# A linear attention and a mixture of sixteen experts in one kernel: thirteen products of ones between two batches of the first expert, and the second expert's first weights asked for earlier

## The chip, the cores and the metric

The kernel runs on one core of a Trainium2 chip. A core has a matrix engine (TensorE, PE in the profile; PEld is its loading of weights), a vector engine (VectorE, DVE), an engine for activations and copies (ScalarE, ACT), a general one (GpSimd, POOL) and SyncE (SP), which here only issues transfers. Transfers run on 16 DMA engines. The engines have queues of their own and wait for one another by semaphores. The metric is the device time of one execution, in microseconds (us).

## The reference

The first half is a recurrent attention over 4 sequences of 768 tokens, 8 heads of 48: a state of 48x48 per head is decayed by a weight per channel, and the outer product of key and value is added. The second half is a layer of experts for the 3072 tokens of 384 values. Each token picks one of 4 groups and one of 4 experts in it, by the greatest logit, and its result is scaled with both softmax weights.

```python
for t in range(S):
    cur = np.einsum('bhd,bhe->bhde', u[None] * kt, vt)
    y[:, :, t] = np.einsum('bhd,bhde->bhe', rt, state + cur)
    state = w[None, :, :, None] * state + np.einsum('bhd,bhe->bhde', kt, vt)
x = attn_out.transpose(0, 2, 1, 3).reshape(B * S, H * D)
g_idx = np.argmax(x @ w_group, axis=1)
...
e_idx = np.argmax(xg @ w_expert[g], axis=1)
...
h = np.maximum(xg[mask_e] @ w1[g, e], 0.0)
out[tok_idx] = combined[:, None] * (h @ w2[g, e])
```

An expert's weights are w1 of 384x1024 and w2 of 1024x384 in 32 bits, 1536 KB each.

## The kernel before, in words

**Attention and routing.** The sequences are worked through in 24 tiles of 128 tokens (six chunks of each of four sequences), in a loop over steps s (L852) whose order on each engine is the order in which the code is written. A tile is turned (`turn`), scored (`scores`), multiplied with the values (`values`) and brought back to rows (`back`) in successive steps. Behind that its logits are computed, and its tokens' expert, gate and place are found (`route`, L377). POOL then scatters the tile's rows by an indirect transfer (L457) into `x_sorted` in device memory, where each expert has a region of its own, in the order in which the tokens come. The last two scatters belong to the last two tiles.

**The experts begin before the routing has ended.** After 16 tiles (s = 21) `pick_first` has chosen the two experts with the most tokens so far; their numbers are loaded into SP as `first` and `second` (L894, L895). SP asks for the first expert's w1 (`load_w1`, L482: four transfers of 384 KB, 32 partitions each), later for the first 128 of its rows (`load_rows(0, ...)`, L933) and its w2 (`load_w2`, L488: one transfer of 1536 KB). The first expert's tokens are worked off in two batches of 128 (items 0 and 1); each of the other experts has one batch of 173 to 240 tokens (items 2 to 16).

**An item.** `columns` (L556) transposes its rows on DVE into `xe`. `up(i, f)` (L585) makes two of the eight row blocks of the hidden layer for f = 0, 2, 4, 6 (matmuls at L596), and ACT applies the rectifier (L600) into `hT`. `down(i, d)` (L605) makes one of three blocks of the result (matmuls at L617) into the tile `po`, and ACT copies it out (L620). ACT copies w2 in four parts into the order in which `down` reads it (`w2_part`, L477, the copies at L480). POOL scatters the results (L656).

**Where the weights lie.** Two places take turns. Place 0 (`w1`, `w2`) holds the first expert. Place 1 is laid over the rings that held k and r in the attention, `kall` and `rall`: the second expert's w1 goes into `kall`, its w2 into `rall`. The last reader of k in `kall` is POOL (L691).

**The order around the change.** PE's order: the last tile's end, `up(0, 4)`, `up(0, 6)`, `down(0, 0)`, `down(0, 1)`, `down(0, 2)`, then for item 1 `up(1, 0)` to `up(1, 6)` and `down(1, 0)`, then `up(2, 0)` and so on, with an item's last two `down` after the next item's first `up`. SP's order: `load_w2(first, 0)`; two of the four row transfers of item 1 (L963; the other two go from ACT) and its keys; four row transfers of item 2 and its keys (L987); the second expert's w1 and w2 (L988); then the third expert's rows and weights. The transfers of `x_sorted` rows to item 1 wait until all scatters into it have landed.

**Products that only use PE.** `warm(n)` (L201) multiplies a 128x128 tile of ones with itself n times into a PSUM bank called `idle`; the kernel calls it twice at its start (8 and 5 times). PSUM banks come in turn from a pool of six (`bank`, L90).

Of the kernel before, what the change touches and what calls it, by code (L numbers as in the profile page):

```python
# [15 lines left out]
P = 128  # L16
# [18 lines left out]
def kernel(  # L35
# [54 lines left out]
    def bank(shape, name):  # L90
        return psum.tile(shape, FP32, tag="bank", name=name)
# [106 lines left out]

    idle = bank([P, P], "idle")

    def warm(n):  # L201
        for _ in range(n):
            nc.tensor.matmul(idle, lhsT=ones, rhs=ones, start=True, stop=True)

# [87 lines left out]
    def turned(m):  # L292
# [5 lines left out]
        )  # L298

    warm(5)  # L300
    backwards(0, nc.vector)
    turned(0)
# [74 lines left out]
    def route(pool, rb, xt, T, sums, number, group, apart=False):  # L377
# [77 lines left out]
        def rows(i):  # L455
# [10 lines left out]
    places = [  # L466
        (wpool.tile([P, KO, F], FP32, name="w1"), wpool.tile([P, FO, DM], FP32, name="w2")),
        (
            kall.rearrange("p j a h d -> p (j a h d)").rearrange("p (k f) -> p k f", f=F),
            rall.rearrange("p j a h d -> p (j a h d)")[:, 0 : FO * DM].rearrange("p (k d) -> p k d", d=DM),  # L470
        ),
    ]
# [9 lines left out]
    def load_w1(e, i):  # L482
        for q in range(P // BL):
            nc.sync.dma_start(
                out=places[i][0][BL * q : BL * (q + 1)], in_=w1f[bass.ds(e, 1), q].rearrange("a p k f -> (a p) k f")
            )

    def load_w2(e, i):  # L488
        nc.sync.dma_start(out=places[i][1], in_=w2f[bass.ds(e, 1)].rearrange("a p k f -> (a p) k f"))

    def load_expert(e, i):

        load_w1(e, i)
        load_w2(e, i)
        return places[i]
# [15 lines left out]
    weights, xgs, xes, keys_of, hTs, yo = {}, {}, {}, {}, {}, {}  # L511

    def width(i):
        return ITEMS[i][2] - ITEMS[i][1]
# [4 lines left out]
    def item_tile(i, shape, name, dtype=FP32, bufs=2):  # L519
        return pools[min(i, 1)].tile(shape, dtype, tag=name, bufs=bufs if i > 0 else 1, name=name)  # L520

    def room(i):
        return P if i == 0 else CAP

    def is_last(i):
        return i == len(ITEMS) - 1

    def padded(n):
        return -(-n // BL) * BL

    def load_rows(i, expert, queue, other=None):

        def tl(shape, name):
            if i < 3:
                return pools[0].tile(shape, FP32, name=f"{name}_{i}")
            return pools[1].tile(shape, FP32, tag=name, bufs=3, name=name)

        n = room(i)  # L540
        xg, key = xgs[i] = tl([P, n // BL, KO, BL], "xg"), tl([P, n // BL, ROW_EXTRA], "key")
        a, w, rows = ITEMS[i][1], padded(width(i)), regions[bass.ds(expert, 1)]
        for q in range(P // BL):
            if other is not None and q % 2:
                of, by = regions[bass.ds(other[0], 1)], other[1]
            else:
                of, by = rows, queue
            by.dma_start(
                out=xg[BL * q : BL * (q + 1), 0 : w // BL].rearrange("t b k d -> t b (k d)"),
                in_=of[:, a : a + w, BL * KO * q : BL * KO * (q + 1)].rearrange("a (b t) d -> t (a b) d", t=BL),  # L550
            )
        p = P if is_last(i) else BL
        n = -(-w // p) * p
        queue.dma_start(out=key[0:p, 0 : n // p], in_=rows[:, a : a + n, DM:XW].rearrange("a (j p) w -> p (a j) w", p=p))

    def columns(i):  # L556
        xg = xgs[i][0]
        w = padded(width(i))
        xe = xes[i] = item_tile(i, [P, KO, room(i)], "xe")
        for ko in range(KO):  # L560
            nc.vector.transpose(xe[:, ko, 0:w].rearrange("p (b t) -> p b t", t=BL), xg[:, 0 : w // BL, ko, :])  # L561
# [43 lines left out]
    def down(i, d, beside=None):  # L605

        w = width(i)
        if d == 0:
            yo[i] = item_tile(i, [P, KO, room(i)], "yo")
            if w < padded(w):  # L610
                nc.vector.memset(yo[i][:, :, w : padded(w)], 0.0)  # L611
        hT, w2 = hTs[i], w2_parts[ITEMS[i][0] % 2]
        po = bank([P, w], "po")
        for fo in range(FO):
            if fo == FO // 2 and beside is not None:
                beside()
            nc.tensor.matmul(  # L617
                po, lhsT=w2[:, fo, d, :], rhs=hT[:, fo, 0:w], start=(fo == 0), stop=(fo == FO - 1)
            )
        nc.scalar.copy(yo[i][:, d, 0:w], po)  # L620
# [231 lines left out]
    for s in range(NT + LAST):  # L852
        pieces = todo.pop(s, [])

        def schedule(n):

            if n not in ROUTED:
                return
            choice, expert, exps, before, gate, place, rows = routing(n)
            if n == NT - 1:  # L860
                choice()
                expert()
                w2_part(0, 6, nc.scalar.copy)
                ending.extend((exps, before, gate, place, rows))
                return
            a = n + 4
            if n < NT - B - 1:
                when = [(a, "choice"), (a + 1, "choice"), (a + 1, "last"), (a + 2, "first")] + 2 * [(a + 2, "last")]
            elif n == NT - B - 1:
                when = [(a, "choice"), (a, "choice"), (a, "last")] + 3 * [(a + 1, "last")]  # L870
            else:
                when = [(a, "choice"), (a, "choice")] + 4 * [(a, "last")]
            for i in range(ROUTED[n]):
                when.append((when[5][0] + (1 + i if n < FOUR * B - 1 else 0), "last"))
            each = [lambda i=i: rows(i) for i in range(ROUTED[n])]
            for (at, place_in), part in zip(when, [choice, expert, exps, before, gate, place] + each):
                if at == s:
                    pieces.append((place_in, part))
                else:
                    todo.setdefault(at, []).append((place_in, part))  # L880

        def run(when):
            for at, part in pieces:
                if at == when:
                    part()

        if s % 2 == 0 and s // 2 + 2 < NP:
            load_pair(s // 2 + 2)
        if s in (3, 5, 7, 9):
            zero_places(s // 2 - 1)  # L890
        if s == FOUR * B + 4:
            pieces.append(("last", pick_first))
        if s == FOUR * B + 5:
            first = expert_of(first_i[0:1, 0:1], (SP,))  # L894
            second = expert_of(first_i[0:1, 1:2], (SP,))  # L895
            load_w1(first, 0)
        if s == NT:
            columns(0)
        run("first")
        if s < NT:  # L900
            turn(s)
            if s == 1:
                turned(1)
                turn_small()
            if s in (1, 2):
                own_sum(0, s - 1, s)
            if s % 2 == 1 and s // 2 + 1 < NP:
                if s > 1:
                    scale_k(s // 2 + 1, nc.gpsimd)
                own(s // 2 + 1, nc.gpsimd)  # L910
        n = s - 4
        if 0 <= n < NT - B:
            row_logits(n)
            schedule(n)
        run("choice")
        if s == NT + 1:
            up(0, 0)
        if s == NT + 2:
            up(0, 2)
        if s == NT + 1:  # L920
            for a in (0, 2, 4):
                w2_part(0, a, nc.gpsimd.tensor_copy)
        if 0 <= s - 3 < NT:
            back(s - 3)
        if 0 <= s - 1 < NT:
            own_scores(s - 1)
        if s == 2:
            scores(1)
        if 0 <= s - 2 < NT:
            values(s - 2)  # L930
        run("last")
        if s == FOUR * B + 5:
            load_rows(0, first, nc.sync)  # L933
            load_w2(first, 0)
            weights[0] = places[0]
        n = s - 3
        if n >= NT - B:
            row_logits(n)
            schedule(n)
        if 0 <= s - 1 < NT and s != 2:  # L940
            scores(s - 1)
        if s % 2 == 0 and 0 < s // 2 < NP:
            own_sum(s // 2)

        if s == 3:
            backwards(2, nc.scalar)
        if s == 4:
            turned(2)
        if s in (2, 4):
            powers(s // 2, nc.scalar)  # L950
        if s == 3:
            span_decay()
        if s == 4:
            check_decay()
# [29 lines left out]
    nc.vector.tensor_copy(left_i, left[:, 0:1])  # L984
    down(0, 1)
    down(0, 2)
    load_rows(2, second, nc.sync)  # L987
    weights[1] = load_expert(second, 1)  # L988
    written.close()
    alive.close()  # L990

# [271 lines left out]
```

## Time and profile before

| what | value |
| --- | --- |
| median of 4 runs | 435.04 us (434.58 to 435.88) |
| profiled execution, its own time | 433.13 us |
| span of the profiled execution | 431.4 us |
| granted clock of TensorE, mean over the span | 0.989 |
| transfers | 86.67 MB, 201 GB/s over the span |
| TensorE busy | 409.1 us (95%) |

The span runs from the first to the last instruction of the program that the profiler recorded; 1.7 us of the execution lie around it. Times in the views are us from the span's start. A line of a timeline gives the start, the length, the engine, the line of the kernel, the operation, output and inputs, the count of records, and in brackets the idle time of the engine before it and what ended it. SPq and ACTq mark the issue of a transfer, not its time on the DMA engines. A line by stretches gives the busy time of each engine in the stretch with the number of its records in brackets, then the granted clock of TensorE (1 is full), the mean share of the 16 DMA engines and what they moved. A 32-bit matmul leaves two records on PE.

### The profile page before, as it was taken

The numbers are of one execution on the slowest core, as the hardware profiler recorded it, in microseconds if no ns is written. First come the engines' busy times: TensorE is split into PE (matmuls) and PEld (weight loads), VectorE is DVE, ScalarE is ACT, GpSimd is POOL, SyncE is SP. The second block draws the span as 40 slices with busy tenths as digits, with TensorE's granted clock in tenths as the row PEclk, the third lists the DMA queues.
The fourth block names the chain that finished last, engine by engine and source line by source line (L and its number), as shares of the span: only waits on it lengthen the run. The fifth ranks groups of instructions, "written<-read, shape, count | busy, mean of one in ns | idle before, by whom it ended". The sixth has DMA issues, their size and how long they took to land. (4 is left out here: it accounts for less than half of the span.)

```text
span 431.4 us, 9878 instructions
## 1 busy us (share of the span) xinstructions
PE 409.1 (95%) x3623; PEld 382.4 (89%) x3623; DVE 183.6 (43%) x620; ACT 215.9 (50%) x505; POOL 202.1 (47%) x214
## 2 busy tenths in 40 slices
PE   6799999999989877999999999999999999999993
PEld 5688888888867677899999999999999999999993
DVE  6666879787948545030312403313213313303211
ACT  2797776767657311335435264263463463365330
POOL 6875567666670733030427235154254255335353
PEclk9999999999998998999999999999999999999998
DMA  9999999981195229999999979899899899999001
GB/s 180 226 234 270 313 246 217 226 155 40 45 231 170 75 92 195 272 267 245 217 257 262 185 222 270 184 242 240 211 251 235 222 241 260 220 264 270 21 23 37
DMA packets 124477, 86.67 MB, mean 201 GB/s; under 512 B 96999, under 2 KB 113566, under 8 KB 124421
## 3 DMA queue, kind: packets, MB, share of 16 engines
q1 hardware_dynamic: 112732, 69.05, 71.8%
q0 software_dynamic: 4960, 9.48, 6.8%
q10 hardware_dynamic: 6728, 7.44, 5.2%
q8 instruction: 30, 0.49, 0.5%
q14 instruction: 27, 0.21, 0.2%
HBM read 70.15 MB, written 16.44 MB: 201 GB/s over the span
## 5 line engine op out<-in xcount | busy, mean ns | idle before, releaser
L656 POOL DMA_INDIRECT out_dram<-yp,ids x104 | 101.1, 972 | 163.9 <-DVE yo L611 128.6
L617 PE MATMUL po<-hT,w_parts 128*128 128x128 f32 (+15 forms) x816 | 139.7, 328 | 1.1 <-ACT hT L600 1.1
L617 PEld LDWEIGHTS po<-hT,w_parts 128*128 128x128 f32 x816 | 133.8, 190 | 2.2 <-ACT hT L600 1.3
L649 DVE STREAM_TRANSPOSE yr<-yo 128x224 f32<-128x224 f32 (+3 forms) x48 | 21.9, 461 | 185.6 <-ACT yo L620 181.2
L596 PE MATMUL ph<-xe,w 128*128 128x128 f32 (+7 forms) x432 | 73.4, 326 | 4.3 <-DVE xe L561 3.4
L596 PEld LDWEIGHTS ph<-xe,w 128*128 128x128 f32 x432 | 70.1, 195 | 5.5 <-issue 5.0
L596 PE MATMUL ph<-xe,kall 128*128 128x240 f32 (+7 forms) x384 | 68.6, 335 | 0.6 <-DMA kall<-in_moe_w_dram 0.6
L596 PEld LDWEIGHTS ph<-xe,kall 128*128 128x128 f32 x384 | 65.4, 190 | 1.3 <-issue 0.7
L600 ACT ACTIVATE hT<-ph 128x256 f32<-128x256 f32 (+15 forms) x68 | 33.3, 494 | 65.5 <-PE ph L596 40.5
L620 ACT COPY yo<-po 128x128 f32<-128x128 f32 (+15 forms) x51 | 16.1, 320 | 89.7 <-PE po L617 58.2
L705 ACT ACTIVATE am<-ident,du 128x128 f32<-128x128 f32 x192 | 58.7, 390 | 1.8 <-DVE du L697 1.5
L480 ACT COPY w_parts<-rall 128x768 f32<-128x768 f32 x32 | 37.9, 1236 | 3.2 <-DMA rall<-in_moe_w_dram 3.2
L735 DVE COPY_PREDICATED am<-later,pa 128x512 f32<-128x512 uint32 x48 | 32.7, 730 | 16.2 <-PE pa L730 7.8
L480 ACT COPY w_parts<-w 128x768 f32<-128x768 f32 x29 | 34.4, 1234 | 2.6 <-DMA w<-in_moe_w_dram 2.6
L457 POOL DMA_INDIRECT x_sorted<-xt,place_i x24 | 23.8, 991 | 24.3 <-DVE rb L822 15.9
L691 POOL TENSOR_TENSOR dg<-rall,kall 128x768 f32<-128x768 f32 (+1 forms) x13 | 22.1, 1699 | 24.0 <-DVE du L697 23.2
L730 PE MATMUL pa<-rT,kT 48*128 48x128 f32 x384 | 29.8, 286 | 1.4 <-issue 1.2
L730 PEld LDWEIGHTS pa<-rT,kT 48*128 48x128 f32 x384 | 24.2, 187 | 4.1 <-issue 2.4
L758 PE MATMUL py<-am,vt 128*64 128x128 f32 x384 | 26.4, 279 | 0.0
L684 POOL TENSOR_TENSOR kh<-kall,T 128x768 f32<-128x768 f32 (+1 forms) x12 | 21.7, 1805 | 7.8 <-PE py L758 3.1
L720 ACT COPY kT<-pk 128x512 f32<-128x512 f32 x24 | 14.0, 583 | 20.9 <-PE pk L716 19.1
L758 PEld LDWEIGHTS py<-am,vt 128*64 128x64 f32 x384 | 20.5, 136 | 4.3 <-issue 3.8
(146 smaller groups left out, 401.5 us busy)
## 6 DMA issues: line engine op xcount, KB each, us to landing
w<-in_moe_w_dram SPq DMA_DIRECT2D x32, 384.0 KB
w<-in_moe_w_dram SPq DMA_DIRECT2D x8, 1536.0 KB
kall<-in_moe_w_dram SPq DMA_DIRECT2D x32, 384.0 KB
rall<-in_moe_w_dram SPq DMA_DIRECT2D x8, 1536.0 KB
x_sorted<-nothing ACTq DMA_DIRECT2D x4, 1544.0 KB
rall<-in_r_dram SPq DMA_DIRECT2D x12, 384.0 KB
vt<-in_v_dram SPq DMA_DIRECT2D x12, 384.0 KB
kall<-in_k_dram SPq DMA_DIRECT2D x10, 384.0 KB
```

The source lines that it names most:

```text
L457: ins = nc.gpsimd.indirect_dma_start(out=xs_dram, out_offset=bass.IndirectOffsetOnAxis(ap=place_i[:, i : i + 1], axis=0), in_=xt[:, i, :], ...
L480: copy(w2_parts[e % 2][:, a : a + 2], w2[:, a : a + 2, :].rearrange("p f (c k) -> p f k c", k=KO))
L596: nc.tensor.matmul(ph[:, q, :], lhsT=w1[:, ko, P * (f + q) : P * (f + q + 1)], rhs=xe[:, ko, 0:w], start=(ko == 0), stop=(ko == KO - 1), s ...
L600: nc.scalar.activation(hTs[i][:, f : f + 2, 0:w], ph, AF.Relu)
L617: nc.tensor.matmul(po, lhsT=w2[:, fo, d, :], rhs=hT[:, fo, 0:w], start=(fo == 0), stop=(fo == FO - 1))
L649: nc.vector.transpose(yr[:, 0:b, :, d], y[:, d, 0:w].rearrange("p (b t) -> p b t", t=BL))
L656: ins = nc.gpsimd.indirect_dma_start(out=out_pieces, out_offset=bass.IndirectOffsetOnAxis(ap=ids[:, j : j + 1], axis=0), in_=yp[:, j], in_ ...
L691: engine.tensor_mul(dg, rts[g % RING][:, a0:a1, :, 0:D], kts[g % RING][:, a0:a1])
L705: nc.scalar.mul(am[:, e, hc, :], ident, dus[n // 2][:, n % 2, h : h + 1])
L730: nc.tensor.matmul(pa[e][:, hc, :], lhsT=kT[rows, hc, :], rhs=rT[rows, hc, :], start=True, stop=True, skip_group_check=True,)
L735: nc.vector.copy_predicated(am[:, e], earlier, pa[e])
L758: nc.tensor.matmul(py[e][DP * o : DP * (o + 1), j, :], lhsT=vt[:, a, 4 * o + 2 * j + e, :], rhs=am[:, e, 2 * o + j, :], start=(c == 0), st ...
```

## The change

Two edits. First, after `down(0, 2)`, PE gets 13 products of ones into a bank of their own, ahead of the first expert's second batch (`up(1, 0)`); `warm` takes the bank as an argument for that. Second, the four transfers of the second expert's w1 into `kall` are written at step s = 24, before anything else of that step but the transposes of the first expert's rows; so they stand on SP's queue right after `load_w2(first, 0)`, ahead of the row and key transfers of items 1 and 2. The transfer of its w2 stays where it was.

```diff
-    def warm(n):
+    def warm(n, idle=idle):
         for _ in range(n):
             nc.tensor.matmul(idle, lhsT=ones, rhs=ones, start=True, stop=True)
...
             load_w1(first, 0)
         if s == NT:
             columns(0)
+            load_w1(second, 1)
         run("first")
...
     down(0, 1)
     down(0, 2)
+
+    warm(13, bank([P, P], "idle"))
     load_rows(2, second, nc.sync)
-    weights[1] = load_expert(second, 1)
+    load_w2(second, 1)
+    weights[1] = places[1]
```

`load_expert` was `load_w1` followed by `load_w2`, and returned the place.

## The prediction

> **What bounds the kernel now.** I read the busy shares first: TensorE (PE) works 409.1 of 431.4 us, so what can be won is PE's idle time and the time in which its clock is low.
>
> ```profile
> span 431.4 us, 9878 instructions
> ...
> PE 409.1 (95%) x3623; PEld 382.4 (89%) x3623; DVE 183.6 (43%) x620; ACT 215.9 (50%) x505; POOL 202.1 (47%) x214
> ```
>
> Then PE's timeline where the change lies, from the first expert's second product to the second expert's first (start, length, then the idle time before and its releaser):
>
> ```profile
> 153.93 5.60 PE L617 MATMUL po<-hT,w_parts 128*128 128x128 f32 x48
> 162.95 6.96 PE L596 MATMUL ph<-xe,w 128*128 128x128 f32 x48 [3.42 <-DVE xe L561]
> 169.74 1.06 PE L617 MATMUL po<-hT,w_parts 128*128 128x128 f32 x8
> 171.90 1.16 PE L617 MATMUL po<-hT,w_parts 128*128 128x128 f32 x8 [1.10 <-ACT hT L600]
> 173.64 5.10 PE L596 MATMUL ph<-xe,kall 128*128 128x240 f32 x24 [0.59 <-DMA kall<-in_moe_w_dram]
> ```
>
> A matmul of 128x128 leaves two records. 48 records take 5.60 us before the wait of 3.42 us and 6.96 us after it. The 1.10 us and the 0.59 us are the two further waits. After 173.64 the table of PE's waits holds one wait more, 0.4 us at the end; the rest of the span is PE without a gap, so what PE gains before 173.64 should reach the end.
>
> Then the stretches of the clock (stretch, length, busy us of PE, PEld, DVE, ACT, POOL; granted clock; DMA share; GB/s):
>
> ```profile
> 124.85:128.26 3.41, 2.08 (x22) 1.33 (x17) 0.02 (x1) 1.49 (x6) 2.76 (x3) 1.00 0.89 265
> 128.26:131.67 3.41, 3.25 (x14) 2.50 (x13) 1.81 (x3) 1.23 (x3) 0.16 (x1) 0.50 0.18 67
> 158.98:162.39 3.41, 0.55 (x5) 0.36 (x4) 0.00 (x0) 0.60 (x3) 0.00 (x0) 1.00 0.38 81
> 162.39:165.81 3.42, 2.86 (x13) 2.89 (x14) 3.18 (x20) 0.00 (x0) 0.14 (x1) 0.50 0.77 173
> 165.81:169.22 3.41, 3.41 (x33) 3.41 (x32) 2.60 (x15) 0.77 (x2) 2.77 (x3) 1.00 1.05 228
> ```
>
> The clock is 0.50 in exactly two stretches of 3.41 us, each behind one in which PE had been busy 2.08 or 0.55 us. The stretch 162.39 to 165.81 lies in the first expert's second batch.
>
> Last, who issues what and when. SP's queue:
>
> ```profile
> 133.82 0.39 SPq L489 DMA_DIRECT2D w<-in_moe_w_dram  x1
> 159.42 0.83 SPq L548 DMA_DIRECT2D xg<-x_sorted  x2
> ...
> 160.95 2.00 SPq L548 DMA_DIRECT2D xg<-x_sorted  x4
> ...
> 163.72 1.85 SPq L484 DMA_DIRECT2D kall<-in_moe_w_dram  x4
> 165.81 0.39 SPq L489 DMA_DIRECT2D rall<-in_moe_w_dram  x1
> ```
>
> ACT where PE waits for it, and DMA (last two columns: share and GB/s) in two stretches:
>
> ```profile
> 171.46 0.66 ACT L600 ACTIVATE hT<-ph 128x256 f32<-128x256 f32 x2 [3.81 <-remote]
> ```
>
> ```profile
> 140.00:142.00 2.00, 2.00 (x21) 1.88 (x20) 1.90 (x8) 0.10 (x1) 0.36 (x1) 1.00 0.00 0
> ...
> 150.00:152.00 2.00, 1.88 (x17) 1.91 (x18) 1.34 (x8) 1.37 (x4) 1.11 (x2) 1.00 0.00 0
> ```
>
> SP issues nothing from 134.2 to 159.4: it stands at the first expert's rows, until the last scattered rows have landed. DMA is empty at 140 to 142 and at 150 to 152.
>
> **The products of ones.** 13 products are 26 records. The 48 records of the second product before the wait took 5.60 us, so one costs 0.117 with its fringe, and the spacing of back-to-back records is 0.111: 26 take 2.9 to 3.0 us. They start when PE goes idle at 159.53 and end at 162.4 to 162.6, in front of 162.95, when the transposed rows come. They cost nothing, with 0.4 us to spare; if the rows came earlier by more, the excess would be paid one for one, at most the whole 2.9. Their bank held a batch that ACT read by 154.4, so they wait for nothing. One bank more is taken from the six, so the third batch of L596 now waits for ACT's copy of the first second-product tile, done at 160.9, some 5 us ahead of its use: nothing.
>
> What they win is the clock. The stretch 158.98 to 162.39 becomes full, and the next is not granted half. At half clock 13 records start between 162.95 and 165.84, 0.211 apart by the trace; at 0.111 they need 1.44 us instead of 2.89. Gain 1.44 us. Bounds from the same two numbers: the stretches need not fall in this place in each execution. A gap of 3.42 us that is split by a boundary can lower one stretch or two. With the fall somewhere between 2.08 us busy (fell) and 2.32 us busy (169.22 to 172.63, did not fall), the loss in before is at least about 1.1 us, when most of the gap is in the first stretch, and at most about 2.8, when both fall. I take 1.44, the row of the profiled execution.
>
> The Trainium skill (TensorE: Matmul & The Clock Gate, Part 1) has the low state follow at least one idle window of about 3.4 us, on windows that run free of the kernel. Read strictly, a gap of 3.42 us would almost never fill a whole window, the clock would mostly not fall, and this part would win 0 instead of 1.44. The trace speaks against the strict reading: the clock fell after a stretch with 2.08 us of work.
>
> **The second expert's first weights, ahead of the rows.** Four issues of 384 KB move on SP past eight issues: two of rows and one of keys of the first expert, four of rows and one of keys of the second. They need kall free (POOL's last read ends at 120.3) and the expert's number, which SP loaded before 117. So SP issues them after 133.82, from about 134.4 to 136.3, in time in which it stands idle; no load of r, k or v is behind them, the last went out at 88.1. The transfer follows the first expert's 1536 KB, which drains by 140. In before these four moved at about 200 GB/s (1.57 MB from about 165 to 173), so they land near 148; the four scatters of 142 to 147 (0.79 MB) share the engines and may make it 152. Nothing that the end waits for moves then: the scatters issued at 155.33 and 156.61 come later. The first expert's second weights are ahead in the same queue; if the two shared the engines evenly, both would be in by 148 (3.1 MB at about 250 GB/s), 1.5 us behind POOL's copy of them at 146.4, whose 1.5 us would be taken out of POOL's 2.5 us of idle time in front of 155.33. Cost nothing; bound above, 1 us on the rows.
>
> It wins the 0.59 us wait, all of it: the rows of the second expert were transposed by 167.4, so nothing else is late there. SP's row issues at 159.42 wait for the scatters as before. The later issues gain: rall goes out about 2 us earlier and finds no 1.57 MB in front of it, so it lands near 170 instead of 180. The order of ACT's weight copies changes from three and one to one, two and one between activations; each is 1.24 us, the activations come no later than before, and PE had no wait there. Nothing is counted for it. Further loads are let go by PE, which is early, and PE never waited for a later one.
>
> **The wait of 1.10 us.** ACT started the third activation at 171.46, 2.9 us after PE's records say its matmuls ended (168.57): its releaser is not told ("remote"). Nothing in the change touches that. It may come again in the same place (0 won, or more lost, next rival), or pass where PE does not need ACT (1.10 won). I take 0.6, the middle, since neither end has a row that decides.
>
> **The sum.** 1.44 + 0.59 + 0.6 = 2.6 us. The profiled execution took 433.13 us (span 431.4 and 1.7 around it), 1.9 us under the median of 435.04. The sum against it gives 430.5; the same difference on the median gives **432.4**, with 430.7 (2.8 + 0.59 + 1.10 won) and 434.5 (only the 0.59) as ends.
>
> **The rivals.** *The late completion takes the gain back.* If PE's completions reach ACT at 171.44 whatever PE did before, PE, early by 1.44, waits 2.5 us instead of 1.10, and only 0.59 us is won: 434.5, no measurable change. For it: the 2.9 us are explained by no instruction. Against: such lateness falls at other times elsewhere (142.7 to 146.6 too, by the same comparison), and so is not bound to this place.
>
> *The early load delays the rows: slower.* Place: the last scatters, between 155.3 and 159.4, and the row transfers behind them. When the first expert's first weights moved beside scatters, rows were issued 2.83 us after the last scatter (128.42 to 131.25), against 1.84 us here (157.58 to 159.42): 1.0 us of price. If the weights stood in front of the rows in full it is up to 7.9 us. A delay over the 3.42 us wait leaves PE idle longer than the products last and brings the low clock back. It decides from 2.6 + 0.9 = 3.5 us of delay, that is, if the weights still move at about 160; I have them done by 152. At 5 us of delay: 437.4. Another page, DMA: Bandwidth & Descriptors, Queues, rings and completion order, says that each DMA engine takes turns between queues packet by packet; if the load were late, that would stretch the scatters too, and the trace has no such overlap at 155 to 159.
>
> *The products outlast the wait: slower.* At half clock 26 records are 5.5 us, 2.1 past the rows; 435.0 - 0.6 + 2.1 = 436.5. Against: the clock is 1.00 from 131.67 on and PE is dense up to 159.53.
>
> **How the numbers follow.** A measurement of this kernel tells 0.2% (0.87 us) from no change. The forecast 0.74, own range 430.7 to 433.9; gain taken back 0.14; rows delayed 0.06; products too long 0.06. Some of the forecast's low end falls within 0.87 us. Faster 0.75, same 0.14, slower 0.11. The range that leaves out 2 in 10 is 430.6 to 435.3.
>
> **What the changed profile would show.** 26 records of L203 from about 159.5, the wait at xe under 0.6 us, no stretch of clock 0.50 near 163; 48 records of the first expert's second batch in about 5.6 us; L484 for kall on SP at about 134.4; DMA busy at 140 to 148; no wait for kall; the rall copies at about 175 without a DMA wait. Wrong it would be if the xe wait ends later than 163, if PE's wait for hT is 2 us or more, or if a wait for weights appears after 190.

## The result, and the profile after

The changed kernel takes 433.07 us in the median of 52 executions (431.15 to 435.43), the kernel before 435.02 in 78 executions beside them. The ratio is 0.9954, with a 95% interval from 0.9943 to 0.9965: faster by 0.46%, 1.5 to 2.5 us. The profiled execution of the changed kernel took 433.82 us, span 432.0.

So the gain is in the medians and not in the two profiled executions, of which the later one is 0.69 us slower. The trace of before is of an execution 1.9 us under its kernel's median; that of after lies 0.75 us over its own. What the two traces can show is the place of each step.

PE's timeline of the changed kernel, over the same work (start, length, and in brackets the idle time before and what ended it):

```profile
154.47 5.61 PE L617 MATMUL po<-hT,w_parts 128*128 128x128 f32 x48
159.91 3.07 PE L203 MATMUL idle<-ones 128*128 128x128 f32 x26
163.24 5.62 PE L596 MATMUL ph<-xe,w 128*128 128x128 f32 x48 [0.26 <-DVE xe L561]
168.70 1.50 PE L617 MATMUL po<-hT,w_parts 128*128 128x128 f32 x12
172.23 0.71 PE L617 MATMUL po<-hT,w_parts 128*128 128x128 f32 x4 [2.02 <-ACT hT L600]
172.78 6.71 PE L596 MATMUL ph<-xe,kall 128*128 128x240 f32 x24
179.32 1.95 PE L617 MATMUL po<-hT,w_parts 128*128 128x128 f32 x16
```

The products fill the wait for the rows (3.42 us before, 0.26 now), the batch behind them takes 5.62 us instead of 6.96, and the wait for `kall` is gone. But the wait for `hT` has grown from 1.10 to 2.02 us, and the second expert's first 24 records take 6.71 us where they had taken 5.10.

Why they do is in the stretches of the clock (length; busy us of PE, PEld, DVE, ACT, POOL; granted clock, DMA share, GB/s):

```profile
158.98:162.39 3.41, 3.41 (x33) 3.41 (x33) 0.00 (x0) 0.60 (x3) 0.00 (x0) 1.00 0.33 79
162.82:166.24 3.42, 3.16 (x28) 3.00 (x27) 3.23 (x20) 0.40 (x2) 0.17 (x1) 1.00 0.70 149
166.24:169.65 3.41, 3.41 (x33) 3.41 (x32) 2.55 (x15) 0.75 (x2) 2.73 (x3) 1.00 0.99 361
169.65:173.06 3.41, 1.39 (x11) 1.19 (x11) 0.00 (x0) 0.47 (x2) 0.97 (x1) 1.00 1.15 252
173.06:176.48 3.42, 3.42 (x10) 2.88 (x9) 0.35 (x1) 0.18 (x1) 0.00 (x0) 0.50 1.04 232
```

The first of these lines takes the stretch of before's table; the changed kernel's own stretch at that place, 159.41 to 162.82, is as full. The low clock was not removed, it moved: out of the first expert's second batch (162.39 to 165.81 before) into the second expert's (173.06 to 176.48), behind the stretch with the longer wait for `hT`.

SP's queue and DMA did as forecast: the four transfers go out at 135.01, DMA is full from 140 to 150 and nearly empty behind that, and the rows go out at 160.10, which is 5.63 us after the down blocks began, against 5.49 before.

```profile
134.38 0.39 SPq L489 DMA_DIRECT2D w<-in_moe_w_dram  x1
135.01 1.97 SPq L484 DMA_DIRECT2D kall<-in_moe_w_dram  x4
160.10 0.83 SPq L548 DMA_DIRECT2D xg<-x_sorted  x2
```

```profile
140.00:142.00 2.00, 2.00 (x26) 1.88 (x23) 1.80 (x9) 0.19 (x1) 0.00 (x0) 1.00 1.10 266
...
146.00:148.00 2.00, 1.33 (x11) 1.06 (x9) 0.00 (x0) 0.00 (x0) 2.00 (x2) 1.00 1.01 206
148.00:150.00 2.00, 1.55 (x14) 0.79 (x13) 0.99 (x7) 1.65 (x7) 2.00 (x3) 1.00 0.95 336
150.00:152.00 2.00, 1.34 (x12) 1.37 (x13) 1.38 (x8) 1.62 (x4) 1.38 (x2) 1.00 0.07 19
```

**What the wait for hT is.** ACT's timeline and POOL's, changed kernel:

```profile
167.56 0.38 ACT L600 ACTIVATE hT<-ph 128x256 f32<-128x256 f32 x1 [0.96 <-PE ph L596]
171.79 0.38 ACT L600 ACTIVATE hT<-ph 128x256 f32<-128x256 f32 x1 [3.85 <-remote]
```

```profile
166.07 0.97 POOL L656 DMA_INDIRECT out_dram<-yp,ids  x1 [7.95 <-DVE yp L651]
167.34 0.97 POOL L656 DMA_INDIRECT out_dram<-yp,ids  x1 [0.30 <-issue]
168.61 0.97 POOL L656 DMA_INDIRECT out_dram<-yp,ids  x1 [0.30 <-issue]
169.89 0.97 POOL L656 DMA_INDIRECT out_dram<-yp,ids  x1 [0.30 <-issue]
```

PE's records say that the fourth up block ended at 168.87; its completion reached ACT at 171.77, 2.9 us later. In before it was the third block, ended at 168.57 and told at 171.44. In both, the news came 0.9 to 1.0 us after POOL's fourth indirect transfer of the first batch's results. I compared, over the whole trace, the ends of the PE instructions that raise the semaphore with the times at which it was recorded as raised, inside the runs of indirect transfers on POOL (transfers less than about 6 us apart count as one run, with 1.3 us behind each) and outside:

| profile | inside: completions | recorded over 1 us late | of these, ACT starts at the raising and not before; latest | outside: completions, recorded over 1 us late |
| --- | --- | --- | --- | --- |
| before | 146 | 47 | 25, 3.4 us | 239, 0 |
| after | 144 | 42 | 22, 3.9 us | 242, 0 |
| early weights alone | 145 | 38 | 18, 3.2 us | 240, 0 |
| products alone | 146 | 43 | 20, 3.2 us | 240, 0 |
| changed kernel, second and third chip (e0, f0) | 152 | 0 | 0 | 234, 0 |

The third column takes for a completion the next raising on record, and some raisings are not on record (in before, 374 are for 385 instructions). So it counts completions that were not late: for 8 of before's 47 an ACT instruction that waits for PE starts within 0.06 us of the product's end, and all that are recorded 6 us late or more (6.3 in before, 8.2 in the products alone) are of this kind. The fourth column counts the cases in which such an ACT instruction starts within 0.05 us of the raising and none starts between the product's end and it; there ACT did get the news late.

That became the question for the experiments: what the products win if the completion that PE needs next has a time of its own.

### The profile page after: what moved, and what is told of

Same layout as the page of the kernel before. It is cut to its first block, busy times and chain, and to the rows that moved or that the text cites. A ratio compares the mean times of both kernels' runs of the same rounds, so it can differ in the third digit from the quotient of the medians.

```text
span 432.0 us, 9930 instructions
## 1 busy us (share of the span) xinstructions
PE 412.5 (95%) x3649; PEld 386.6 (89%) x3649; DVE 183.8 (43%) x620; ACT 215.8 (50%) x505; POOL 202.0 (47%) x214
## 5 line engine op out<-in xcount | busy, mean ns | idle before, releaser
L617 PE MATMUL po<-hT,w_parts 128*128 128x128 f32 (+15 forms) x816 | 139.7, 328 | 2.0 <-ACT hT L600 2.0
L617 PEld LDWEIGHTS po<-hT,w_parts 128*128 128x128 f32 x816 | 133.8, 190 | 3.1 <-ACT hT L600 2.2
L596 PE MATMUL ph<-xe,w 128*128 128x128 f32 (+7 forms) x432 | 71.8, 322 | 1.1 <-issue 0.8
L596 PEld LDWEIGHTS ph<-xe,w 128*128 128x128 f32 x432 | 68.7, 190 | 2.1 <-issue 1.2
L596 PE MATMUL ph<-xe,kall 128*128 128x240 f32 (+7 forms) x384 | 70.2, 340 | 0.0
L596 PEld LDWEIGHTS ph<-xe,kall 128*128 128x128 f32 x384 | 66.6, 193 | 1.0
```

What stands on the lines that cost most here:

```text
L596: nc.tensor.matmul(ph[:, q, :], lhsT=w1[:, ko, P * (f + q) : P * (f + q + 1)], rhs=xe[:, ko, 0:w], start=(ko == 0), stop=(ko == KO - 1), s ...
L617: nc.tensor.matmul(po, lhsT=w2[:, fo, d, :], rhs=hT[:, fo, 0:w], start=(fo == 0), stop=(fo == FO - 1))
```

## The experiments

They ran in three groups, each on one chip. The first chip is like the one of the result (before takes 433.81 us there, and completions come late). On the other two, no completion of PE in any profile was over 0.1 us late and before takes 427.64 and 427.33 us; ratios are therefore always to before on the same chip. Beside the ratio I give the stage, a time in the profiled execution: from the start of the first batch's down blocks to the start of the second batch's second down block (both L617 on PE), which stands behind the second expert's first two up blocks (24.65 us in before: 153.93 to 178.58; 24.85 in after: 154.47 to 179.32).

### The early weights alone (e1)

```diff
-    warm(13, bank([P, P], "idle"))
```

> The early weights without the products. First theory (two gains that add up: 1.4 to 1.8 us from the clock, 0.6 us from the weights): 0.6 us faster than before (0.14%), the 0.59 us wait for kall gone, the clock low for one stretch near 163 as in before. Second theory (PE's completions reach ACT late, at about 171.5 whatever PE did): the wait for hT stays at about 1.1 us and the gain is the same 0.6 us. Third theory (the two edits need each other: each alone leaves the other's limit in force): also 0.6 us, since in before the second expert's batch can't start sooner than 173.05 without the products. So this run fixes the size of one term; it tells the theories apart together with the products alone.

Ratio 0.9917 (0.989 to 0.9945), median 431.34 us against 433.81; stage 23.18 us. That is 2.47 us won, where every theory had about 0.6: the expectation was missed by a factor of four.

```profile
153.67 5.61 PE L617 MATMUL po<-hT,w_parts 128*128 128x128 f32 x48
162.58 7.22 PE L596 MATMUL ph<-xe,w 128*128 128x128 f32 x48 [3.30 <-DVE xe L561]
169.64 1.50 PE L617 MATMUL po<-hT,w_parts 128*128 128x128 f32 x12
171.44 0.71 PE L617 MATMUL po<-hT,w_parts 128*128 128x128 f32 x4 [0.30 <-ACT hT L600]
171.99 5.03 PE L596 MATMUL ph<-xe,kall 128*128 128x240 f32 x24
176.85 1.95 PE L617 MATMUL po<-hT,w_parts 128*128 128x128 f32 x16
```

The second expert's batch starts 18.32 us after the down blocks; with the products it starts 18.31 us after them (172.78 less 154.47). So in the traced executions on this kind of chip 13 products win nothing at that point: they let PE be early, and it waits 2.02 us instead of 0.30 for the late `hT`. Then they lose 1.68 us (6.71 against 5.03), since the low clock now falls on the larger batch. The stage is 1.47 us shorter than before: 1.39 us less of waiting for `hT` and `kall`, the rest small differences of both signs.

### The products alone (e2)

```diff
-            load_w1(second, 1)
...
-    load_w2(second, 1)
-    weights[1] = places[1]
+    weights[1] = load_expert(second, 1)
```

> The products without the early weights. First theory (gains add up): 1.4 us faster than before (0.3%). Third theory (they need each other): the second expert's first batch can't start before its weights land, 173.5 in the profile of before, so the 1.4 us turn into a longer wait for kall (0.6 us plus what the first batch ends earlier, 2 us or so in all); within 0.2% of before, and perhaps slower, if the longer wait brings the low clock back in a stretch of 3.41 us behind it (1.6 us).

Ratio 1.0029 (1.0008 to 1.0049): slower. Stage 27.22 us (153.71 to 180.93).

```profile
168.18 1.50 PE L617 MATMUL po<-hT,w_parts 128*128 128x128 f32 x12
171.70 0.71 PE L617 MATMUL po<-hT,w_parts 128*128 128x128 f32 x4 [2.02 <-ACT hT L600]
174.31 6.79 PE L596 MATMUL ph<-xe,kall 128*128 128x240 f32 x24 [1.90 <-DMA kall<-in_moe_w_dram]
180.93 1.95 PE L617 MATMUL po<-hT,w_parts 128*128 128x128 f32 x16
```

The wait for `hT` is 2.02 us as in the changed kernel, so the early weights don't cause it; the wait for the weights is 1.90 us, and the low clock follows (24 records in 6.79 us). The first theory's 1.4 us fell here. The third theory held for this half: on this chip the products need the early weights. The early weights do not need the products.

### Twice the products (e3)

```diff
-    warm(13, bank([P, P], "idle"))
+    warm(26, bank([P, P], "idle"))
```

> 26 products in place of 13, with the early weights: 6.1 us of products from about 159.9, so they end 2.5 us behind the rows. First theory: everything behind them is 2.5 us later, 2.5 us slower than the changed kernel (about 0.5 us, 0.1%, slower than before). Second theory (late completions at a time of their own, near 171.7): the wait of 2.02 us for hT in the changed kernel's profile is taken up by the products, so the second expert's batch starts within 0.6 us of the changed kernel's 172.78, and without the low clock at 173 to 176 that the wait brought; then as fast as the changed kernel or up to 1 us faster.

Ratio 0.9955 (0.9934 to 0.9976), as the changed kernel's 0.9954, though the products outlast the rows; stage 23.78 us (154.65 to 178.43).

```profile
160.09 5.97 PE L203 MATMUL idle<-ones 128*128 128x128 f32 x52
165.90 5.52 PE L596 MATMUL ph<-xe,w 128*128 128x128 f32 x48
171.26 1.06 PE L617 MATMUL po<-hT,w_parts 128*128 128x128 f32 x8
172.57 1.16 PE L617 MATMUL po<-hT,w_parts 128*128 128x128 f32 x8 [0.26 <-ACT hT L600]
173.57 5.03 PE L596 MATMUL ph<-xe,kall 128*128 128x240 f32 x24
```

The up batch ends 16.61 us after the start of the down blocks (171.26 less 154.65), against 14.23 in the changed kernel, 2.4 us later; the wait for `hT` is only 0.26 us, and the clock stays full in the stage. Against the changed kernel about 3 us of further products cost nothing, because PE would have waited and then run at half clock. Against no products at all, e1 in the same group, they cost 1.15 us (432.49 against 431.34 us).

### Products in the second wait as well (e4)

```diff
                 go_on()
+                if i == 1:
+                    warm(9, bank([P, P], "idle"))
                 down(i, 0)
```

> The changed kernel with 9 more products of ones (2.0 us) between the first expert's last up batch and its first down block, where the profile of the changed kernel shows 2.02 us of waiting for hT and after it a stretch at half clock (173.06 to 176.48, in which 24 records take 6.71 us against 5.10). If that wait is there in the timed runs too (second theory): the products lie in the wait, the clock is held, and it is 0 to 1.6 us faster than the changed kernel (ratio to before 0.992 to 0.995). If the wait belongs to the profiled execution alone: 2.0 us slower than the changed kernel, no faster than before (ratio 1.000).

Ratio 0.9919 (0.9891 to 0.9947), median 431.21 us, as forecast for a wait that is there in the timed runs (0.992 to 0.995); stage 22.89 us (153.46 to 176.35), the shortest on this chip.

```profile
158.90 3.07 PE L203 MATMUL idle<-ones 128*128 128x128 f32 x26
162.23 5.62 PE L596 MATMUL ph<-xe,w 128*128 128x128 f32 x48 [0.26 <-DVE xe L561]
167.69 2.17 PE L203 MATMUL idle<-ones 128*128 128x128 f32 x18
169.70 1.95 PE L617 MATMUL po<-hT,w_parts 128*128 128x128 f32 x16
171.49 5.03 PE L596 MATMUL ph<-xe,kall 128*128 128x240 f32 x24
```

2.17 us of additional products made the kernel no slower than the changed one, so the wait is there in the timed runs and not in the profiled one alone. No stretch of this execution up to the end has a low clock; its mean over the 6 runs is 0.993, against 0.985 in the 22 runs of before in this group.

### The changed kernel again, and three variants (e0, e6, e7, e5)

The scatter later (e6; e7 has it without the products):

```diff
             keys_in(0)
-            pieces_out(0)
             keys_in(1)
...
                         if not left_over:
                             pieces_out(i - 1)
+                        elif i == 2:
+                            pieces_out(0)
```

The down block behind the second expert's first up block (e5):

```diff
                 up(i, 0)
+                if i == 2:
+                    down(1, 0)
...
                 go_on()
-                down(i, 0)
+                if i > 1:
+                    down(i, 0)
```

> The changed kernel once more, beside the three that follow, so that they are compared with it under the same conditions. Expected: ratio to before 0.994 to 0.997, and in the profile the wait for hT of about 2.0 us that ends about 11.8 us after the first batch's down blocks end.

> The changed kernel with the scatter of the first batch's results (four indirect transfers on POOL, 166.07 to 170.86 in the changed kernel's profile) written after the second expert's second up block and one down block, so that it starts some 3 us later, behind the last up block of the first expert. Theory now: while POOL issues indirect transfers, PE's completions reach ACT late (in the profile of before all 47 that came over 1 us late fell in such a run of transfers or within 1.3 us of one, none of 239 outside). Then the wait for hT falls from 2.0 us to under 0.3, the second expert's batch starts 2.0 us earlier, and the clock stays full: 2 to 3.6 us faster than the changed kernel, ratio to before 0.986 to 0.990. Rival (the lateness belongs to something else that falls 11.8 us after the down blocks, the weights' transfer or code loading): the wait stays at 2.0 us and the time at that of the changed kernel.

> The early weights alone, with the scatter later and no products. If the products pay once the late completions are out of the way: slower than the run before this one in the list by the clock's 1.4 to 1.8 us, and faster than the early weights alone by no more than their 0.30 us wait for hT. If the products never pay: as fast as that run.

> The changed kernel with the first expert's first down block of the second batch behind the second expert's first up block, so that PE has 2.5 us of other work before it needs the late hT; the scatter stays. By the theory of late completions the wait is covered: no wait for hT over 0.3 us, full clock, 2 to 3.6 us faster than the changed kernel. If the products themselves cost the time (for instance by what they do to the clock afterwards), no gain.

On this chip the changed kernel's ratio is 0.9885 (0.986 to 0.991), median 423.05 us, not the 0.994 to 0.997 that was expected. Its profile has no wait for `hT`, though POOL scatters at the same place of the order (159.20 to 164.00); ACT's fourth activation is released by PE, 0.96 us behind the third:

```profile
152.37 3.07 PE L203 MATMUL idle<-ones 128*128 128x128 f32 x26
156.39 5.62 PE L596 MATMUL ph<-xe,w 128*128 128x128 f32 x48 [0.95 <-DVE xe L561]
161.85 1.95 PE L617 MATMUL po<-hT,w_parts 128*128 128x128 f32 x16
163.64 5.03 PE L596 MATMUL ph<-xe,kall 128*128 128x240 f32 x24
```

```profile
162.05 0.38 ACT L600 ACTIVATE hT<-ph 128x256 f32<-128x256 f32 x1 [0.96 <-PE ph L596]
```

With nothing late there is nothing to cure: the scatter later gives 0.9896 (0.9869 to 0.9923), the down block later 0.9895 (0.9868 to 0.9922), both the changed kernel's time. So they won nothing over it, and their theory, which is for a chip with late completions, was not tested; e6's ratio falls in its forecast range because the changed kernel itself lies there on this chip. The run without products (e7) gives 0.993 (0.9903 to 0.9957), 425.0 us: 1.95 us slower than the changed kernel and 1.78 slower than e6, as expected if the products pay (1.4 to 1.8).

### The same on a third chip (f0 to f3)

> The changed kernel, as the base of the three that follow. On a chip whose PE completions come late while POOL issues indirect transfers: ratio 0.994 to 0.997 and a wait for hT near 2 us; on one where they never do (as on the chip of the group before): ratio 0.987 to 0.990 and no wait for hT.

> The changed kernel with the first batch's scatter later, once more. Where completions come late: no wait for hT over 0.5 us, clock full behind it, 2 to 3.6 us faster than the changed kernel beside it. Where they don't: the same time as the changed kernel, within 0.3 us, as in the group before.

> The changed kernel with the first down block of the second batch behind the second expert's first up block, once more. Where completions come late: the wait for hT is covered by 2.5 us of matmuls, 2 to 3.6 us faster than the changed kernel beside it, by a way that leaves the scatter where it is. Where they don't: the same time as the changed kernel.

> The early weights without the products, beside the changed kernel. Where completions come late: 0.9 to 2 us faster than the changed kernel, since half clock makes PE arrive at the late hT when it is there, and the products only move the low clock behind the wait. Where they don't: 1.4 to 2.3 us slower than the changed kernel, which is then what the products win (the run without products and with the scatter later was 1.95 us slower than the changed kernel there).

Again no completion was late, and all four came as expected for such a chip. The changed kernel: 0.9897 (0.988 to 0.9914), 423.04 us. The scatter later: 0.99 (0.9881 to 0.9918). The down block later: 0.9903 (0.9885 to 0.992). The early weights alone: 0.9944 (0.9925 to 0.9962), 425.12 us, 2.08 us slower than the changed kernel. PE in the changed kernel (f0, two lines), then in the early weights alone (f3):

```profile
156.67 5.62 PE L596 MATMUL ph<-xe,w 128*128 128x128 f32 x48 [1.09 <-DVE xe L561]
162.13 1.95 PE L617 MATMUL po<-hT,w_parts 128*128 128x128 f32 x16
```

```profile
147.72 5.60 PE L617 MATMUL po<-hT,w_parts 128*128 128x128 f32 x48
157.64 7.22 PE L596 MATMUL ph<-xe,w 128*128 128x128 f32 x48 [4.32 <-DVE xe L561]
164.70 1.95 PE L617 MATMUL po<-hT,w_parts 128*128 128x128 f32 x16
166.48 5.03 PE L596 MATMUL ph<-xe,kall 128*128 128x240 f32 x24
```

Here the products win what they were reckoned to: the up batch from start to start of the next line takes 7.06 us without them and 5.46 with them (f0: 156.67 to 162.13), 1.60 us; with 0.33 us by which the rows came later in this execution that is 1.93 of the 2.08 us. The mean clock is 0.991 without and 0.995 with the products; 0.0042 of 423 us is one half-clock stretch of 3.41 us (1.7 us of full clock).

## Why the prediction was right, and where its steps failed

Direction and range held: 432.4 forecast, 433.07 measured, 2.6 us of gain against 1.95 (1.5 to 2.5). That the number came so near is in part luck. Of the 2.6 us, 2.0 were for the products and the wait for `hT`; in the traces of chips with late completions the second expert's batch starts no earlier with the products than without them (18.31 against 18.32 us), and the early weights, priced at 0.59, won 2.47 us alone in e1. Two of the three signs that the prediction named for being wrong came true: the wait for the rows ended at 163.24, behind its 163 (though 8.77 us after the down blocks began, against 9.02 before), and the wait for `hT` was 2.02 us, where 2 or more was the sign. And its low end is mis-added: 435.04 less 2.8, 0.59 and 1.10 is 430.55, not 430.7.

- *The products fit the wait.* 2.9 to 3.0 us forecast, 3.07 measured with the fringe, and 0.26 us left over. Right.
- *The clock, 1.44 us.* The up batch fell from 6.79 us (start to start) to 5.46: 1.33 us. The size was right; on chips without late completions it was 1.60 us. But on the chip of the result it didn't reach the end: PE came early to a completion with a time of its own.
- *"I take 0.6, the middle".* This is the step that failed. The 1.10 us wait did not shrink, it grew to 2.02 us: 0.9 us lost in the place of 0.6 won. The rival named the mechanism and its price almost to the number (2.5 us, if told at a fixed time), and its argument against, that such lateness falls elsewhere too and so isn't bound to this place, was wrong. In these profiles it falls only in POOL's runs of indirect transfers or just behind them, and one lies here.
- *What neither had: the clock behind the longer wait.* The table of stretches showed the low clock behind a stretch with 2.08 us of work and one with 0.55, and I applied it to the first wait only. The second one brought it back, 1.61 us on the 24 records.
- *The early weights, 0.59 us, no cost.* Placement, landing by 148 and the unharmed rows came as reckoned. Alone they win more than that, 1.47 us of stage in e1, since PE's slower batch, at half clock, meets the late `hT` almost in time and then finds the weights there.
- *The rival "the early load delays the rows".* The load did hold up scatters: the 0.8 MB of rows that moved from 142 to 148 before move from 146 to 150 now, behind the weights (packets of the software queue in the two traces). But four more scatters come after these before the rows may go, and the rows went out only 0.14 us later relative to PE. It did not decide.
- *The rival "the products outlast the wait".* In e3 they end the up batch 2.4 us later, at no cost against the changed kernel where completions are late. Its price of one for one was wrong there.

Why the medians show about 2 us when the traced stages differ by 0.2: e1's profiled execution (431.43) and its median (431.34) agree, and it lies 1.70 us under before's profiled one, as stage (1.47) and start of the down blocks (0.26) say. That leaves before's profiled execution as the odd one, 1.9 us under its median. The mean clock does not tell why. It is 0.989 in that profile and 0.985 over the 22 runs of before in the first group, a difference of about one more half-clock stretch; but among these 22 the time does not follow the clock (the six at 0.988 and 0.989 took from 432.79 to 435.82 us). No trace shows what the other executions of before lose; a gap of 3.42 us that lowers two stretches, as the prediction reckoned for its bound, is one possibility. That stays open.

Open too is the cure on a chip with late completions: the scatter later and the down block later only ran where there was nothing late. Of the versions tried there, the early weights alone (0.9917) and the products in both waits (0.9919) stand before the changed kernel (0.9954), whose interval touches theirs only at its edge; it ran beside its own runs of before, not in their group. Without late completions the changed kernel is the best that was run, level with e5 and e6.

## What to carry to other kernels

Work that keeps PE's clock up in one wait is worth what the next wait leaves of it: follow the stretch to the next thing PE needs from another engine, and ask whether that has a time of its own. A wait whose releaser the profile does not tell deserves a comparison over the whole trace (here ends of matmuls against the raising of their semaphore, sorted by what POOL does) before it is priced at the middle. And take away the transfer that stands behind the wait first: on the chip with late completions the products without the early weights were slower than before, and on all three chips of the experiments the early weights without the products were faster (on the second with the scatter later).

## What was not expected of the hardware

While POOL issues a run of indirect transfers, PE's completions reached ACT late on the chips of the result and of the first group: of about 145 in such runs 18 to 25 came over 1 us late with ACT starting at the raising, the latest 3.2 to 3.9 us, and none of about 240 outside. On two other chips none was late at all, with the same program. By the down blocks' start (153.46 to 154.65 there, 146.92 to 147.72 here) those are about 7 us ahead already. That the transfers cause it was inferred from this sorting and, for the `hT` of the first expert's second batch, from its end 0.9 to 1.0 us behind the last transfer; it was not shown by moving them on a chip that has it.

The clock fell behind stretches of 3.41 us that were far from idle. The Trainium skill (TensorE: Matmul & The Clock Gate, Part 1) has it fall after an idle window of about that length; here 1.39 us of PE work in the stretch (after, 169.65) did not keep it, nor 2.38 us in the run with 26 products, in which the next stretch was at half:

```profile
124.69:128.10 3.41, 2.38 (x24) 1.58 (x20) 0.00 (x0) 1.42 (x5) 2.77 (x3) 1.00 0.84 257
128.10:131.51 3.41, 2.82 (x20) 2.18 (x18) 1.98 (x3) 1.23 (x3) 0.15 (x1) 0.50 0.18 65
```

In e1 a stretch with 2.15 us (157.13 to 160.54) was followed by full clock. So PE's busy time alone, as the profile models it, gives no sharp bound between 2.1 and 2.4 us, where the prediction took one between 2.08 and 2.32.
